# Four sets of chunk buffers, a bonus added by TensorE, staged rows of r, and one block a chunk in a recurrent-attention and two-layer kernel

## The chip, the core and the metric

The kernel runs on one core of a Trainium2 chip. The time is device microseconds of that core, and lower is better. A page and a trace of one profiled execution of the kernel before are at hand. The engines are called PE (TensorE), DVE (VectorE), ACT (ScalarE), POOL (GpSimd) and SP (SyncE, which here issues nearly all DMAs).

## The reference

Three stages in fp32: a linear recurrence over 768 tokens in 4 batches and 8 heads of 48, then two dense layers over the 3072 rows that it gives.

```python
B, H, S, D = 4, 8, 768, 48
for t in range(S):
    kt, vt, rt = k[:, :, t], v[:, :, t], r[:, :, t]
    cur = einsum('bhd,bhe->bhde', u[None] * kt, vt)          # the bonus of the token itself
    y[:, :, t] = einsum('bhd,bhde->bhe', rt, state + cur)
    state = w[None, :, :, None] * state + einsum('bhd,bhe->bhde', kt, vt)
x = y as rows (3072, 384)
x = ((x @ w1) * (x @ w2)) @ w3 @ w_mid                        # 384 -> 1024 -> 384
h = x @ w_in                                                  # 384 -> 1024
solu = h * softmax(h)
ln = (solu - mean) / sqrt(var + 1e-6) * g_ln
out = ln @ w_out                                              # 1024 -> 384
```

## The kernel before, in words

**Chunks.** The recurrence is cut into 24 chunks of 128 tokens; chunk n holds tokens of batch n % 4, and four chunks make a group c (0 to 5). For a chunk, r and k come transposed (`rT`, `kT`, loads "R" and "K", 48 x 512 each in two DMAs) and k and v by rows ("k" and "v"). `prep_R` and `prep_K` scale them by powers of w (`tab`). `a_chunk` (PE) multiplies them to a 128 x 128 matrix per head, and DVE copies the causal half of it into the tile `asb` under a mask ("ev", `copy_predicated`). On the diagonal of `asb` stands the bonus, one number per token and head. It is made in two ways: for chunks 0 to 8 (`n < NR`) DVE or POOL multiplies the transposed tiles (`prep_rk`), PE sums them with u (`bonus_mm`), and ACT copies the eight sums out; for later chunks POOL multiplies rows of r by u and k (`prep_ru`, `prep_ruk`), and DVE sums them (`bonus`). `diag` then writes the bonus into the diagonal of `asb`, on DVE or ACT. `y_chunk` (PE) multiplies `asb` by v and, from the second group on, adds r times the state; ACT and DVE split the result into a high and a low half ("yh", "yl") for exact products later. `st_chunk` (PE) and DVE advance the state.

**Dense layers.** Every fp32 product of the layers is three fp32r matmuls of high and low halves (`mm3`, L165 to L167). `s1_a` and `s1_b` give one 128-wide slice ft of the two products with w1 and w2 for the four chunks of a group (nine 512-column matmuls each), `s2` (nine again) multiplies their product by wc = w3 @ w_mid, which `w3_out` makes on the chip in eight parts "W". A second phase (from the first `ps_h` on) runs the second layer.

**Weights.** 24 units of weights are converted into halves on the chip. Each takes seven instructions on ACT, DVE and POOL (the functions from `cv_m` to `cv_h`, and `split`), of which DVE mostly has three (L429, L439, L448).

**Order.** Up to the end of the second group (`NG = 2`) a small planner, class `Plan`, orders all work: it holds a cost and a set of predecessors for each named step, starts the step that can start first, and breaks ties by the longest way to the end plus a bonus from the table `PRI`. Where PE would be idle before the first `s1_a`, it puts matmuls that compute nothing (`keep_warm`, L562). Each engine then works through its own list in order. After that, from c = 2 on, loops written by hand run `s1_a`, `s1_b`, `s1_gh`, `s1_gl`, `s2` for each ft, and `slot` puts the two halves of a chunk between them, in every ft one: an even slot has `bonus`, `diag`, `a_chunk`, an odd one `y_chunk` and `st_chunk`.

**Buffers.** There are two sets of `kT`, `rT` (`kTs`, `rTs`), so the loads of chunk n wait until chunk n - 2 has been used, two tiles `asb` up to chunk 8 and one after it, two staging buffers for weight units (`CB`), and a tile pair `wch`, `wcl` for wc that stands empty until the first part W.

Of the kernel before, what the change touches and what calls it, by code (L numbers as in the profile page):

```python
# [104 lines left out]
def tile_rwkv_bilinear_solu(  # L105
# [15 lines left out]
    g_ln: bass.AP,  # L121
    out: bass.AP,
# [22 lines left out]
    wch = const.tile([P, KF, DM], F32R, name="wch")  # L145
    wcl = const.tile([P, KF, DM], F32R, name="wcl")
# [47 lines left out]

    def flush():
        while later:
            later.pop(0)()


    def load_chunk(n, which="KRkrv"):  # L200
# [3 lines left out]
        for nm in which:  # L204
            if nm in T_d:
                src, tiles, dst = T_d[nm]
                t = dst[n] = tiles[n % len(tiles)]
                for o in range(2):
                    nc.sync.dma_start(t[o * DP:o * DP + D], src[b, c, o])
            else:  # L210
                if nm == "r" and not rows:
# [3 lines left out]
                    uall = u.rearrange("h d -> (h d)").partition_broadcast(P)  # L215
                    nc.sync.dma_start(rows["u"], uall.rearrange("p (h d) -> p h d", h=H))
# [14 lines left out]
    def prep_ru(n, e=nc.gpsimd):  # L231
        e.tensor_mul(rkv[n, "r"], rkv[n, "r"], rows["u"])
# [14 lines left out]
    def bonus_mm(n):  # L247
# [9 lines left out]
        later.append(evac)  # L257
# [5 lines left out]
    def asb_of(n):  # L263
        return asbs[n % 2 if n < N2 else 0]
# [47 lines left out]
    def y_chunk(n):  # L312
# [6 lines left out]
        for m, (hs, es) in enumerate(cuts):  # L319
            if c > 0:  # L320
                for j in range(HQ):
# [7 lines left out]
                    )  # L329
            if m < KM - 1:  # L330
                for j in range(HQ):
                    h = hs.start + j
                    nc.tensor.matmul(
                        ps[j * E0:(j + 1) * E0, m, :], lhsT=vt[:, h, es], rhs=asb_of(n)[:, h, :], start=c == 0, stop=True
                    )
            else:
                for o in range(2):
                    for j in range(NP):
# [3 lines left out]
                            start=c == 0 and o == 0, stop=o == 1,  # L342
# [4 lines left out]
    def st_chunk(n):  # L347
# [5 lines left out]
        ps = psa.tile([P, NP, D], F32, name="ps_s", tag="psa")  # L353
# [159 lines left out]
    def w3_out(ft):  # L513
# [3 lines left out]
        return split(ps, wch[:, ft, :], wcl[:, ft, :])  # L517
# [31 lines left out]
    for i, t in enumerate(kTs + rTs):  # L549
        (nc.vector if i % 2 else nc.gpsimd).memset(t, 0.0)  # L550
    nc.vector.memset(u2, 0.0)
    for o in range(2):
        nc.scalar.dma_start(
            u2[o * DP:o * DP + D, :, o], u.rearrange("(p o) d -> o d p", o=2)[o], allow_slow_non_contiguous=True
        )

    make_identity(nc, ident)
# [7 lines left out]
    nc.vector.memset(kpad[1], 0.0)  # L565
# [674 lines left out]
```

## Time and profile before

| | |
|---|---|
| median of 3 runs | 678.31 us (676.22 to 678.32) |
| the profiled execution | 679.14 us, of which the span from first to last instruction is 677.4 us |
| mean granted TensorE clock | 0.997 |
| PE busy | 665.0 us, 98% |
| DVE, ACT, POOL busy | 404.9, 299.3 and 252.0 us |

The profiled execution lies 0.83 us above the median. Busy PE counts the matmuls that compute nothing too, and a matmul's end is modelled, so 98% says where the limit is and not that PE does useful work all that time. An fp32 matmul of 128 columns shows as two records in the trace and as one row in the order of instructions.

### The profile page before, as it was taken

The numbers are of one execution on the slowest core, as the hardware profiler recorded it, in microseconds if no ns is written. First come the engines' busy times: TensorE is split into PE (matmuls) and PEld (weight loads), VectorE is DVE, ScalarE is ACT, GpSimd is POOL, SyncE is SP. The second block draws the span as 40 slices with busy tenths as digits, with TensorE's granted clock in tenths as the row PEclk, the third lists the DMA queues.
The fourth block names the chain that finished last, engine by engine and source line by source line (L and its number), as shares of the span: only waits on it lengthen the run. The fifth ranks groups of instructions, "written<-read, shape, count | busy, mean of one in ns | idle before, by whom it ended". The sixth has DMA issues, their size and how long they took to land.

```text
span 677.4 us, 12433 instructions
## 1 busy us (share of the span) xinstructions
PE 665.0 (98%) x4828; PEld 567.0 (84%) x4828; DVE 404.9 (60%) x730; ACT 299.3 (44%) x625; POOL 252.0 (37%) x253
## 2 busy tenths in 40 slices
PE   8999999999999999999999999999999999999996
PEld 8888778997777888888877887878999999999996
DVE  7798996666665433333344276537666666676653
ACT  3567965662322222322242366444544444444442
POOL 4576743331003455555584356332211222211210
PEclk9899999999999999999999999999999999999999
DMA  6567786453443122222121233000000000000001
GB/s 174 189 218 251 229 263 209 159 187 93 141 135 97 59 66 68 67 82 62 59 72 19 109 130 117 0 1 13 24 24 13 24 24 24 25 23 25 13 24 39
DMA packets 43379, 60.13 MB, mean 89 GB/s; under 512 B 6193, under 2 KB 31794, under 8 KB 43314
## 3 DMA queue, kind: packets, MB, share of 16 engines
q1 hardware_dynamic: 42898, 59.27, 27.8%
q8 instruction: 40, 0.66, 0.4%
q14 instruction: 25, 0.20, 0.1%
q10 hardware_dynamic: 416, 0.00, 0.0%
HBM read 50.34 MB, written 8.91 MB: 87 GB/s over the span
## 4 chain that ended last, share of the span: by engine, by line
PE 72%; DVE 8%; DMA 5%; POOL 5%; ACT 5%; issue 3%; SPq 0%; DVEq 0%; POOLq 0%; ACTq 0%
PE ps_h L165 5%; PE ps_h L167 5%; PE ps_h L166 5%; PE ps_o L167 5%; PE ps_o L166 5%; PE ps_o L165 5%; PE ps_x L165 4%; PE ps_bb L165 4%; PE ps_x L167 3%; PE ps_x L166 3%; PE ps_p L810 3%; PE ps_aa L165 3%; POOL cvm L433 3%; PE ps_bb L167 3%; PE ps_bb L166 3%
## 5 line engine op out<-in xcount | busy, mean ns | idle before, releaser
L647 POOL TENSOR_TENSOR gl<-g,gh 128x512 fp32r<-128x512 f32 x32 | 50.2, 1570 | 104.2 <-ACT gh L642 93.7
L433 POOL TENSOR_TENSOR cvm<-cvm,cvq 128x384 int32<-128x384 int32 (+1 forms) x54 | 64.3, 1197 | 58.8 <-ACT cvq L420 31.4
L788 POOL TENSOR_TENSOR rs<-vs,nhalf 128x1 f32<-128x1 f32 x24 | 13.0, 541 | 171.9 <-DVE vs L786 171.9
L165 PE MATMUL ps_o<-woh,pt 128*128 128x384 f32 x192 | 64.3, 335 | 0.0
L166 PE MATMUL ps_o<-wol,pt 128*128 128x384 f32 x192 | 64.3, 335 | 0.0
L167 PE MATMUL ps_o<-woh,pt 128*128 128x384 f32 x192 | 64.2, 334 | 0.0
L165 PE MATMUL ps_bb<-x,w2h 128*128 128x512 f32 x144 | 59.3, 412 | 0.0
L165 PE MATMUL ps_h<-wih,x2h 128*128 128x512 f32 x144 | 58.6, 407 | 0.7 <-ACT x2c L678 0.7
L769 ACT ACTIVATE e<-ps_h,nm 128x1024 f32<-128x1024 f32 x24 | 26.8, 1117 | 73.3 <-DVE nm L766 73.3
L165 PE MATMUL ps_aa<-x,w1h 128*128 128x512 f32 x144 | 58.1, 403 | 0.2
L636 DVE TENSOR_TENSOR g<-ps_bb,a 128x512 f32<-128x512 f32 x48 | 33.0, 687 | 40.7 <-PE ps_bb L167 40.7
L165 PE MATMUL ps_x<-gh,wch 128*128 128x512 f32 x144 | 57.0, 396 | 0.0
L167 PE MATMUL ps_x<-gh,wcl 128*128 128x512 f32 x144 | 56.3, 391 | 0.5 <-DVE wcl L448 0.5
L279 ACT COPY a<-ps_aa 128x512 f32<-128x512 f32 x44 | 25.6, 582 | 70.3 <-PE ps_aa L167 68.9
L167 PE MATMUL ps_h<-wih,x2l 128*128 128x512 f32 x144 | 56.6, 393 | 0.0
L167 PE MATMUL ps_bb<-x,w2l 128*128 128x512 f32 x144 | 56.4, 392 | 0.0
L167 PE MATMUL ps_aa<-x,w1l 128*128 128x512 f32 x144 | 56.3, 391 | 0.0
L166 PE MATMUL ps_bb<-x,w2h 128*128 128x512 f32 x144 | 56.3, 391 | 0.0
L166 PE MATMUL ps_aa<-x,w1h 128*128 128x512 f32 x144 | 56.2, 390 | 0.0
L166 PE MATMUL ps_h<-wil,x2h 128*128 128x512 f32 x144 | 56.2, 390 | 0.0
L166 PE MATMUL ps_x<-gl,wch 128*128 128x512 f32 x144 | 56.1, 390 | 0.0
L766 DVE TENSOR_REDUCE nm<-ps_h 128x1 f32<-128x1024 f32 x24 | 29.4, 1224 | 38.8 <-PE ps_h L167 38.8
(147 smaller groups left out, 1577.4 us busy)
## 6 DMA issues: line engine op xcount, KB each, us to landing
cvs<-in_w_T_dram SPq DMA_DIRECT2D x16, 512.0 KB, 4.1
cvs<-in_w_dram SPq DMA_DIRECT2D x16, 384.0 KB, 4.0
kT<-in_k_T_dram SPq DMA_DIRECT2D x48, 96.0 KB, 2.5
rT<-in_r_T_dram SPq DMA_DIRECT2D x48, 96.0 KB, 2.7
v_in<-in_v_dram SPq DMA_DIRECT2D x24, 192.0 KB, 3.0
k_in<-in_k_dram SPq DMA_DIRECT2D x24, 192.0 KB, 2.5
out_dram<-o SPq DMA_DIRECT2D x24, 192.0 KB, 1.8
gd<-g SPq DMA_DIRECT2D x16, 256.0 KB, 3.2
```

The source lines that it names most:

```text
L165: nc.tensor.matmul(dst, lhsT=ah, rhs=bh, start=start and i == 0, stop=False)
L166: nc.tensor.matmul(dst, lhsT=ah, rhs=bl, start=False, stop=False)
L167: nc.tensor.matmul(dst, lhsT=al, rhs=bh, start=False, stop=stop and i == last)
L279: (e.copy if e is nc.scalar else e.tensor_copy)(dst, src)
L433: nc.gpsimd.tensor_tensor(mi, mi, q, op=ALU.add)
L636: nc.vector.tensor_mul(gt[c, ft], pb, at[c, ft])
L647: e.tensor_sub(gl, g, f32(gh))
L766: nc.vector.tensor_reduce(out=nm, in_=ph, axis=AX.XY, op=ALU.max, negate=True)
L769: nc.scalar.activation(e, ph, AF.Exp, bias=nm, scale=1.0, accum_out=sm)
L788: nc.gpsimd.tensor_tensor(rs, vs, pq[0]["nhalf"], op=ALU.pow)
L810: nc.tensor.transpose(ps[:, j, :], pv[:, kf * P:(kf + 1) * P], ident)
```

## The change

Line numbers in the order of instructions are those of the respective file: L298 `a_chunk`, L251 `bonus_mm`, L356 `st_chunk`, L327, L333, L340 `y_chunk`, L562 `keep_warm`, L273 `diag`, L302 ev before are L361, L299, L425, L390, L401, L408, L635, L336, L365 after. L397 (identity times `vb`) and L308 (`vb`) are new. The tile named `early` is the area that holds all the early tiles.

1. **Four sets.** An area `early`, which later becomes wc (tag "wx"), holds two more sets of `kT`, `rT`, two more `asb`, and small tiles. Chunks below `NE = 8` rotate over four sets; the parts W may start only when chunks 0 to 7 and the bonus sums of chunks 5 to 8 are done (`free`).
2. **Bonus by TensorE.** For chunks 0 to 3 (`NV = 4`) there is no `diag`: DVE multiplies v by the eight sums from `bonus_mm` (two instructions, `evac_v`), and `y_chunk` adds the product with twelve matmuls against the identity.
3. **Rows of r for chunks 5 to 8.** `NR` goes from 9 to 5, so these four chunks take the way of the later ones, with r and u by rows in `early`.
4. **Staging and start.** Three staging buffers (`CB = 3`); w and u come as one small laid-out input `wu` in one DMA in place of four, the tiles are cleared by other engines in another order, `pw` moves into `early`, and `zero` is a tile of its own (before, it was an element of `rT1`, whose load so waited for ACT's clearing).
5. **One block a chunk** in the loops from c = 2 on: `block` does `y_chunk` and `st_chunk` of chunk n and `bonus`, `diag`, `a_chunk` of chunk n + 1 in one place, after `s1_gl` of every second ft (of every ft in c = 4); `st_chunk` takes the PSUM tile of `ps_aa`.
6. Other numbers in the planner's table, so another order up to the end of the second group.

```diff
-PRI = {'W.0': 20, **{f'yl{n}': 400 - 20 * n for n in range(4)}, **{f'st{n}': 310 for n in range(4)}}
+PRI = {
+    'W.0': 20, 'yl0': 503, 'yl1': 388, 'yl2': 393, 'yl3': 341, 'st0': 289, 'st1': 406, 'st2': 386, 'st3': 283, 'l_22': 37,
...
-CB = 2
+CB = 3
-NR = 9
-W0 = 19
+NR = 5
+NV = 4
+NT = 0
+NQ = 9
+NE = 8
+W0 = 15
+T0 = 8.1
...
+    early = const.tile([P, 2 * KF * DM], F32, name="early", tag="wx")
...
+    def open_wc():
+        if not wc:
+            t = const.tile([P, 2, KF, DM], F32R, name="wc", tag="wx")
+            wc["h"], wc["l"] = t[:, 0], t[:, 1]
...
+    for i in range(2):
+        kTs.append(early_tile(NP, P))
+        rTs.append(early_tile(NP, P))
...
+    def slot(n):
+        return n % 4 if n < NE else n % 2
...
-                t = dst[n] = tiles[n % len(tiles)]
+                t = dst[n] = tiles[slot(n)]
...
+        def evac_v():
+            vb = vbs[n % 2].rearrange("p h d -> p (h d)")
+            for es in (slice(0, E0), slice(E0, D)):
+                nc.vector.tensor_mul(
+                    vb[:, H * es.start:H * es.stop].rearrange("p (h d) -> p h d", h=H), rkv[n, "v"][:, :, es],
+                    ps.unsqueeze(2).to_broadcast([P, H, es.stop - es.start]),
+                )
...
-        later.append(evac)
+        later.append(evac_v if n < NV else evac)
...
+            elif n < NV:
+                vb = vbs[n % 2].rearrange("p h d -> p (h d)")
+                for j in range(HQ):
+                    lhsT = vb[:, (m * HQ + j) * E0:(m * HQ + j + 1) * E0]
+                    nc.tensor.matmul(ps[j * E0:(j + 1) * E0, m, :], lhsT=lhsT, rhs=ident, start=True, stop=False)
...
+    def block(n):
+
         flush()
...
+        more = n + 1 < NCH
+        if more:
+            bonus(n + 1)
+        y_chunk(n)
+        st_chunk(n, psf.tile([P, NP, D], F32, name="ps_s", tag="ps_aa"))
+        flush()
+        if more:
+            diag(n + 1)
+            a_chunk(n + 1)
+            prep_vrem(n + 1)
+            prep_state(n + 1)
+            flush()
+        load_chunk(n + 3, "Kkrv")
+        load_chunk(n + 2, "R")
+        prep(n + 2)
...
+    free = [f"{x}{n}" for n in range(NE) for x in "YS"] + [f"red{n}" for n in range(NR, NQ)]
...
-            f"W.{ft}", {"T": 4.25}, ready["m"] + ready["w"][2 * ft:2 * ft + 2] + [f"W.{ft - 1}"], wout,
+            f"W.{ft}", {"T": 4.25}, ready["m"] + ready["w"][2 * ft:2 * ft + 2] + [f"W.{ft - 1}"] + free, wout,
...
             s1_a(c, ft)
             flush()
-            mid()
+            if late:
+                cvstep()
             s1_b(c, ft)
             flush()
             s1_gh(c, ft)
             s1_gl(c, ft)
+            if cn < NCH and (ft % 2 == 0 or c == NC - 2):
+                block(cn)
+                cn += 1
```

The first place is PE's list just before the first matmul of the dense layers, `ps_aa`. Before, chunks 2 and 3 stand there with idle-time matmuls (`ps_warm`) between them:

```order
L562 MATMUL ps_warm<-ident 128x128 x12
...
L251 MATMUL ps_b<-u_79,rk 128x2 x4
L562 MATMUL ps_warm<-ident 128x128 x3
L333 MATMUL ps_y<-asb,v_in 32x128 x8
L340 MATMUL ps_y<-asb,vrem 32x128 x8
...
L562 MATMUL ps_warm<-ident 128x128 x7
L356 MATMUL ps_s<-v_in,kpad_84 64x48 x8
...
L356 MATMUL ps_s<-v_in,kpad_85 64x48 x8
L251 MATMUL ps_b<-u_79,rk 128x2 x4
L165 MATMUL ps_aa<-x,w1h 128x512
```

After the change the same stretch, from the bonus sums of chunk 3 to the first `ps_aa`, has the identity matmuls and no `ps_warm`:

```order
L299 MATMUL ps_b<-wv,rk 128x2 x4
L397 MATMUL ps_y<-ident,early 32x128 x4
L401 MATMUL ps_y<-early,v_in 32x128 x4
...
L408 MATMUL ps_y<-early,vrem 32x128 x8
L425 MATMUL ps_s<-v_in,kpad_84 64x48 x8
L425 MATMUL ps_s<-v_in,kpad_83 64x48 x8
...
L425 MATMUL ps_s<-v_in,kpad_84 64x48 x8
L191 MATMUL ps_aa<-x,w1h 128x512
```

Over the whole list up to the first `ps_aa` the rows of `ps_warm` go from 56 to 26 matmuls, and `y_chunk` of chunks 0 to 3 from 16 matmuls to 28. From there to the first `ps_h`, `ps_b` goes from 16 matmuls (four chunks) to none, and nothing else changes in number.

The second place is DVE's list at chunk 1, ahead of the first weight unit. Before, `diag` (L273) and a product for chunk 2 stand between two masked copies:

```order
L302 COPY_PREDICATED asb<-mask,ps_a_259 128x4x128
L273 COPY_PREDICATED asb<-ident,s 128x1024
L229 TENSOR_TENSOR kpad_84<-k_in,tabk 128x8x48
L243 TENSOR_TENSOR rk<-kT_82,rT_80 128x512
L448 TENSOR_TENSOR x<-ps_y,x 128x3x128
L302 COPY_PREDICATED asb<-mask,ps_a_325 128x4x128
```

After, `vb` (L308) stands in its place, and both products of chunk 2 with the table come early, on tiles of the third set:

```order
L365 COPY_PREDICATED asb<-mask,ps_a_253 128x4x128
L291 TENSOR_TENSOR rk<-early 128x512
L308 TENSOR_TENSOR early<-v_in,ps_b 128x256
L308 TENSOR_TENSOR early<-v_in,ps_b 128x128
L271 TENSOR_TENSOR early<-early,tab 128x512
L274 TENSOR_TENSOR early<-early,tab 128x512
L519 TENSOR_TENSOR x<-ps_y,x 128x3x128
L365 COPY_PREDICATED asb<-mask,ps_a_323 128x4x128
```

Up to the low half of chunk 3 (`yl3`), which the first `ps_aa` needs, DVE's list loses three rows of `diag`, one `rk` and one weight half (L448), and gains one product with the table and four pairs of L308. From there to the last weight half that the first part W needs it goes from 108 instructions to 122, among them four sums over rows of r; PE's list in the same stretch goes from 20 slices of the dense layer (`s1_a` or `s1_b`) to 23.

The third place is PE's list in the hand-written loop. Before, the two halves of a chunk stand apart, each between dense matmuls:

```order
L167 MATMUL ps_aa<-x,w1l 128x512
L327 MATMUL ps_y<-rT_80,spad 32x128 x4
...
L356 MATMUL ps_s<-v_in,kpad_84 64x48 x8
L165 MATMUL ps_bb<-x,w2h 128x512
...
L167 MATMUL ps_aa<-x,w1l 128x512
L298 MATMUL ps_a_3293<-rT_81,kT_83 128x128
...
L165 MATMUL ps_bb<-x,w2h 128x512
```

After, they are one run of fp32 matmuls between `ps_bb` and `ps_x`:

```order
L193 MATMUL ps_bb<-x,w2l 128x512
L390 MATMUL ps_y<-rT_79,spad 32x128 x4
...
L425 MATMUL ps_s<-v_in,kpad_83 64x48 x8
L361 MATMUL ps_a_3271<-rT_80,kT_82 128x128
...
L191 MATMUL ps_x_2722<-gh,wc 128x512
```

Between the first `ps_aa` and the first `ps_h` the runs of fp32 matmuls (chunk work) between fp32r ones go from 49 to 37: from the third group on from 23 to 12, ahead of it from 26 to 25. Everything from the first `ps_h` on stands in the same order as before.

## Rows read from the trace of the kernel before

**Rows 1.** Page: span, busy time, and PE in 40 equal slices.
```profile
span 677.4 us, 12433 instructions
PE 665.0 (98%) x4828; PEld 567.0 (84%) x4828; DVE 404.9 (60%) x730; ACT 299.3 (44%) x625; POOL 252.0 (37%) x253
...
PE   8999999999999999999999999999999999999996
```

**Rows 2.** Stretches: busy us of each engine (instructions), granted clock, DMA share, GB/s.
```profile
8.77:37.57 28.80, 27.38 (x382) 24.88 (x381) 23.45 (x42) 13.34 (x40) 15.27 (x13) 0.94 0.68 209
37.57:101.00 63.43, 62.99 (x618) 49.66 (x618) 59.29 (x111) 48.96 (x130) 41.18 (x39) 1.00 0.77 240
37.57:445.77 408.20, 406.19 (x3200) 331.36 (x3200) 232.60 (x378) 178.66 (x409) 190.90 (x157) 1.00 0.38 118
445.77:677.40 231.63, 225.06 (x1219) 204.39 (x1217) 143.42 (x289) 103.04 (x170) 41.38 (x71) 1.00 0.06 22
```

**Rows 3.** Timeline of PE to the first dense matmul: start, us, operation, [idle before].
```profile
2.36 7.19 PE L562 MATMUL ps_warm<-ident 128*128 128x128 f32 x38 [2.36 <-POOL ident masks.py:199]
...
20.14 1.02 PE L251 MATMUL ps_b<-u,rk 128*128 128x2 f32 x8 [1.42 <-DVE rk L243]
...
24.65 3.14 PE L562 MATMUL ps_warm<-ident 128*128 128x128 f32 x24
...
32.69 1.83 PE L562 MATMUL ps_warm<-ident 128*128 128x128 f32 x14
...
37.57 0.48 PE L165 MATMUL ps_aa<-x,w1h 128*128 128x512 f32 x1
```

**Rows 4.** Timeline of PE around one `a_chunk` and one `bonus_mm`.
```profile
43.37 0.39 PE L166 MATMUL ps_aa<-x,w1h 128*128 128x512 f32 x1
43.59 0.39 PE L167 MATMUL ps_aa<-x,w1l 128*128 128x512 f32 x1
43.91 1.16 PE L298 MATMUL ps_a<-rT,kT 64*128 64x128 f32 x16
45.00 0.50 PE L165 MATMUL ps_bb<-x,w2h 128*128 128x512 f32 x1
45.34 0.39 PE L166 MATMUL ps_bb<-x,w2h 128*128 128x512 f32 x1
...
47.18 0.95 PE L251 MATMUL ps_b<-u,rk 128*128 128x2 f32 x8
47.99 0.49 PE L165 MATMUL ps_aa<-x,w1h 128*128 128x512 f32 x1
```

**Rows 5.** Timeline of DVE to the first dense matmul.
```profile
8.77 0.69 DVE L243 TENSOR_TENSOR rk<-kT,rT 128x512 f32<-128x512 f32 x1
...
11.87 1.30 DVE L273 COPY_PREDICATED asb<-ident,s 128x1024 f32<-128x1024 int32 x1
13.07 1.75 DVE L223 TENSOR_TENSOR kT<-kT,tab 128x512 f32<-128x512 f32 x1
...
19.30 0.69 DVE L243 TENSOR_TENSOR rk<-kT,rT 128x512 f32<-128x512 f32 x1 [1.57 <-DMA rT<-in_r_T_dram]
19.91 0.55 DVE L448 TENSOR_TENSOR x<-ps_y,x 128x384 fp32r<-128x384 f32 x1
...
22.67 0.35 DVE L362 TENSOR_TENSOR st<-ps_s,w 128x192 f32<-128x192 f32 x1
...
28.92 1.34 DVE L302 COPY_PREDICATED asb<-mask,ps_a 128x512 f32<-128x512 int32 x2 [1.93 <-PE ps_a L298]
```

**Rows 6.** Waits of SP's DMA queue up to 40 us: total, times, longest.
```profile
SPq L209 <- PE ps_a L298: 6.8, 4, 3.3
...
SPq L209 <- ACT vrem L279: 2.1, 1, 2.1
```

**Rows 7.** Timeline of POOL up to 21 us.
```profile
12.09 2.17 POOL L226 TENSOR_TENSOR rT<-rT,tab 128x512 f32<-128x512 f32 x1 [6.67 <-DVE rk L243]
...
20.07 1.27 POOL L223 TENSOR_TENSOR kT<-kT,tab 128x512 f32<-128x512 f32 x1 [4.39 <-DVE rk L243]
```

**Rows 8.** Timeline of POOL in the loop, the first and last of one chunk's five products.
```profile
241.47 1.29 POOL L223 TENSOR_TENSOR kT<-kT,tab 128x512 f32<-128x512 f32 x1
...
246.01 1.06 POOL L235 TENSOR_TENSOR r_in<-r_in,k_in 128x384 f32<-128x384 f32 x1
```

**Rows 9.** Page, DMA issues: KB each, median us to landing.
```profile
rT<-in_r_T_dram SPq DMA_DIRECT2D x48, 96.0 KB, 2.7
```

More of the change, by code (lines that the diff above doesn't have):

```diff
@@ L121, in tile_rwkv_bilinear_solu @@
     g_ln: bass.AP,
+    wu: bass.AP,
     out: bass.AP,
@@ L193, in tile_rwkv_bilinear_solu, with same @@
     later, rows, rowx = [], {}, ExitStack()
+    def slot(n):
+        return n % 4 if n < NE else n % 2
+    def same(n):
+        return max([m for m in range(n) if slot(m) == slot(n)], default=-1)
     def flush():
@@ L231, in prep_ru @@
     def prep_ru(n, e=nc.gpsimd):
-        e.tensor_mul(rkv[n, "r"], rkv[n, "r"], rows["u"])
+        e.tensor_mul(rkv[n, "r"], rkv[n, "r"], rows_e[2] if n < NQ else rows["u"])
     def prep_ruk(n, e=nc.gpsimd):
@@ L255, in evac, with kpad_mm @@
             copy(e, bon[n], ps)
-        later.append(evac)
+        def evac_v():
[6 more added lines that the diff above has]
+        later.append(evac_v if n < NV else evac)
+    def kpad_mm(n):
+        ps = psf.tile([P, NP, P], F32, name="ps_k", tag="ps_bb")
+        for p in range(NP):
+            nc.tensor.transpose(ps[:, p, :], kT[n][:, p, :], ident)
+        later.append(lambda e: copy(e, kpad[n % 2].rearrange("t (p o) d -> t p (o d)", o=2), ps))
     def bonus(n):
@@ L352, in st_chunk @@
         kp, vt = kpad[n % 2], rkv[n, "v"]
-        ps = psa.tile([P, NP, D], F32, name="ps_s", tag="psa")
+        if ps is None:
+            ps = psa.tile([P, NP, D], F32, name="ps_s", tag="psa")
         for h in range(H):
@@ L548, in tile_rwkv_bilinear_solu, with clear @@
     nlim = NU
[L549 to L555, printed above, removed]
+    def clear(e, *tiles):
+        for t in tiles:
+            if e is nc.scalar:
+                nc.scalar.copy(t, zero.unsqueeze(2).to_broadcast(list(t.shape)))
+            else:
+                e.memset(t, 0.0)
+    clear(nc.vector, kTs[0], rTs[0])
+    clear(nc.gpsimd, kTs[1], rTs[1])
+    clear(nc.scalar, kTs[2], rTs[2], kTs[3], rTs[3])
     make_identity(nc, ident)
@@ L996, in tile_rwkv_bilinear_solu @@
             )
-    prio = dict(PRI, **{f"l_{i}": UB * (NU - i) for i in range(NU)})
+    prio = dict({f"l_{i}": UB * (NU - i) for i in range(NU)}, **PRI)
     todo = plan.order(3, prio, {f"A{n}": f"Y{n - 1}" for n in range(1, NA)})
-    clock, idle = 8.8, True
+    clock, idle = T0, True
     for t, name, e, end, fn in todo:
@@ L1210, in rows @@
         return _np.concatenate([x.reshape(-1, FF) for x in (a[0:4, 0:32], a[4:8, 0:32], a[:, 32:])])
+    wu = _np.zeros((2, 64, 3, H // 2), i["w"].dtype)
+    wu[:, :, 0] = 1
+    wu[:, :D, 0] = i["w"].reshape(H // 2, 2, D).transpose(1, 2, 0)
+    wu = wu.reshape(2, 64, 3 * (H // 2))
+    for o in range(2):
+        wu[o, :D, H // 2 + o::2] = i["u"].reshape(H // 2, 2, D)[:, o].T
     laid = {
```

151 lines of the change are left out of this document (74 added, 77 removed), and 3 rows, old and new, of the table PRI.

## The prediction

> **What bounds the kernel now.** I read the page first: PE is busy 98% of the span, in nearly every slice [rows 1], so nothing that DVE, ACT or POOL does later than the start can matter unless it makes PE wait. The stretches say where PE is the limit. From the first dense matmul at 37.57 us to the second phase at 445.77 PE is busy 406.19 of 408.20 us; the second phase takes the remaining 231.63 us and is not touched [rows 2]. Only the 37.57 us before the first `ps_aa` are not PE's: there much of its busy time is `ps_warm`, which computes nothing, 38 records at the start, 24 at 24.65, 14 at 32.69 [rows 3]. The end is thus the sum of two things: when the first `ps_aa` starts, and how much PE has to do from there to the end.
>
> What holds the first `ps_aa` back is the chain of chunks 0 to 3, mostly on DVE: in the 28.80 us from its first product at 8.77 to the first dense matmul DVE is busy 23.45 [rows 2]. Two of its waits carry most of the other 5.35 us: 1.57 for the load of `rT` of chunk 2, and 1.93 for the `a_chunk` that follows from it [rows 5]. The load itself was late because SP held it behind `a_chunk` of an earlier chunk, which was reading the same buffer: 6.8 us in four waits, and 2.1 us more behind ACT's clearing [rows 6].
>
> **The start.** The sum goes against the profiled execution (679.14 us, 0.83 over the median); the result is taken off the median.
>
> The single load of w and u: two SP issues become one of 12 columns, and the clearing is spread. I take 0.4 us (one SP issue of two), between 0 and 0.8. DVE's first product then starts at 8.4.
>
> DVE's work from there to `yl3`: three `diag` of 1.30, one `rk` of 0.69 and one weight half of 0.55 leave, one product of 0.68 comes [rows 5], which is 4.5 less. The four pairs that make `vb` are not in the trace. They read PSUM, 256 and 128 columns; the nearest rows that do so have 384 columns (0.55) and 192 (0.35) [rows 5]. On the line through these two, 256 columns take 0.42 and 128 take 0.28, so a pair takes 0.70, between 0.55 (if broadcasting costs nothing and the small one less than the line) and 0.90; four are 2.8. DVE so does 23.45 - 4.5 + 2.8 = 21.75 us. `diag` is replaced on PE by twelve matmuls in each of four `y_chunk`, in all 96 records of some 0.06 us by the 128-column `a_chunk` (16 in 1.09 us, [rows 4]): 6.5 us of PE time, but in place of `ps_warm`, which had at least 24 and 14 records in 3.14 and 1.83 us there [rows 3]. They cost nothing as long as DVE is later than PE; without that cover they would cost the 6.5 us.
>
> Waits: with four sets the loads of chunks 2 and 3 wait for no matmul, so the 1.57 goes, and with it most of the 1.93 and of the waits for sums that follow. I keep 0.8 of the 5.35 for the latency from PE to DVE. The first `ps_aa` then comes at 8.4 + 21.75 + 0.8 = 31.0 in place of 37.57: **6.6 us earlier**. Ends: all of the waiting stays (35.5, 2.1 earlier), or none and no POOL collision either (29.1, 8.5 earlier).
>
> **PE's work after the start.** Four `bonus_mm`, for chunks 5 to 8, leave: from 47.18 to the next matmul at 47.99 one takes 0.81 [rows 4], four take **3.2 us**. What takes their place (rows of r times u and k, and a sum) goes to POOL and DVE; POOL is busy 41.18 of 63.43 us there and the DMA queues have a share of 0.77 [rows 2], so five more loads of 192 KB lie beside other work.
>
> Switching between fp32r and fp32 matmuls costs PE time. Within a slice a matmul starts 0.22 to 0.23 after the last. The last one before `a_chunk` holds PE for 0.32 (43.59 to 43.91), and the first one after it for 0.34 (45.00 to 45.34) [rows 4]: 0.2 us for each run of chunk work between dense matmuls. There are 12 fewer such runs, 11 of them in the loop, where the two halves of a chunk become one: **2.4 us**. Nothing is added on PE. The cover for the other edits of the loop is PE's own queue: `st_chunk` now takes the tile of `ps_aa`, which the next `s1_a` writes, but nine `s2` matmuls stand between, and the sum that empties the tile takes 0.35 on DVE [rows 5].
>
> **What is given back.** Up to 101 us, shortly before the first part W, DVE was already busy 59.29 of 63.43 us [rows 2]; its list there grows from 108 instructions to 122, at the same mean to 67.0 us. PE has three slices more (27 matmuls of 0.23) and four `bonus_mm` and two switches less: 63.4 + 6.2 - 3.6 = 66.0. So both are full, DVE by 1.0 us more than PE, and any wait of DVE can become a wait of PE. The bounds: nothing (if DVE's new instructions are shorter than its mean), or the 1.0 and all of the 4.1 us that DVE idled in that stretch, 5.1. I take **1.5 us**, nearer to nothing, since the parts W only move behind slices that PE has ready. That W must wait for the last reader of `early` is hidden by the same slices.
>
> Sum: 6.6 + 3.2 + 2.4 - 1.5 = 10.7 us. 679.14 - 10.7 = 668.4, and against the median of 678.31: **667.5 us**.
>
> **Rivals.**
>
> *DVE and POOL block each other.* POOL's product at 12.09 took 2.17 us where a like one takes 1.27 [rows 7], and DVE's product beside it took 1.75 against 0.69 [rows 5]: 1.06 us of DVE lost in one meeting. In the new order POOL has `rk` and products for chunks 1 to 3 while DVE has six products that read two SBUF tiles. By the Trainium skill (SBUF — State Buffer, section "SBUF: two separate sides") DVE and GpSimd take a shared pair of ports as an exclusive lock, against each other when DVE reads two SBUF inputs and GpSimd reads SBUF too; the pair of rows above agrees with it. That speaks against a plan that moves work to POOL. Three meetings more cost 3.2 us of the start, and in the full stretch behind it the 5.1 us would go whole: 6.6 - 3.2 + 5.6 - 5.1 = 3.9 us, **674.4 us**. Against it: only one of DVE's products met POOL in this way before.
>
> *The start is bound by something else.* If `a_chunk`, the weight units or the loads keep DVE waiting as long as before, the first `ps_aa` comes at 35.5: 2.1 + 5.6 - 1.5 = 6.2 us, **672.1 us**. A PE that idles before the first `ps_aa` belongs here: after the pause of 1.42 us at 20.14 [rows 3] the granted clock of the whole stretch was 0.94 [rows 2], and such a fall costs more if it falls on dense matmuls.
>
> *All pauses go.* If the start reaches its lower end, nothing is given back and the 2.0 us in which PE is idle up to 445.77 [rows 2] vanish: 8.5 + 5.6 + 2.0 = 16.1 us, **662.2 us**.
>
> *The block makes PE wait (slower).* In `block` the sum over r of chunk n + 1 stands on DVE ahead of the low half of `y` and of the sum that empties the `ps_aa` tile, and it waits for POOL's last product of that chunk. Those five products take 5.6 us (241.47 to 247.07, [rows 8]) and follow a load of `rT` that lands in 2.7 us [rows 9] and is issued at the end of the block before; the last is so ready some 7.5 us after it. In c = 2 and 3 the next block is two ft away (over 12 us), so there is slack; in c = 4 it is one ft away (27 matmuls of 0.23, 6.2 us), so DVE waits 1.3 us, while PE needs the tile only after the block and `s2`, over 5 us later. From 11 us of waiting on, 1 us in each of 11 blocks, the gain is gone; at 1.5 us in each the time would be 667.5 + 16.5 = **684 us**.
>
> **How the numbers follow.** The forecast's own range is 663.5 to 671, chance 0.57. DVE against POOL 0.17, the start bound elsewhere 0.10, all pauses gone 0.09, slower 0.04, 0.03 is left for a time near no change. The range of 8 in 10 goes from 661 to 674. About 0.3% (2 us) is what a measurement here can tell from no change: faster by more 0.92, within it 0.04, slower 0.04.
>
> **What would show it.** The first `ps_aa` at 30 to 32 us; DVE busy some 22 us from its first `rk` to there with under 2 us of waits, none for a load of `rT`; no `diag` on DVE before it; pairs of L308 at 0.7 us. From the first `ps_aa` to the first `ps_h` about 404 us in place of 408.2, and from there to the end 231.6 as before. It would be wrong if PE shows pauses between 31 and 100 us that end with DVE, or in the loop before `ps_aa` behind `ps_s`, or if the first `ps_aa` comes after 34 us.

## The result and the profile after

The kernel after takes 668.72 us (median of 4 runs, 667.36 to 670.17), the kernel before on the same chip 677.26 (675.64 to 678.32): ratio 0.9864, 95% interval 0.9834 to 0.9893. The profiled execution took 670.03 us. One execution among those below, 679.35 us of h0, lies over 1.5% above the fastest of its kernel and is left out of h0's ratio.

The page of the kernel after (span, busy time) stands against [rows 1]:

```profile
span 668.2 us, 12402 instructions
PE 653.4 (98%) x4832; PEld 558.6 (84%) x4832; DVE 410.2 (61%) x727; ACT 299.1 (45%) x616; POOL 267.4 (40%) x274
```

PE is still the limit. It is busy 11.6 us less, but `ps_warm` is part of that; from the first `ps_aa` to the first `ps_h` it is busy 400.87 us in place of 406.20. The stretches of the kernel after, in the columns of [rows 2], cut at DVE's first product (10.01), the first `ps_aa` (32.58), the first part W (`ps_wc`, 98.94) and the first `ps_h` (436.39):

```profile
10.01:32.58 22.57, 21.55 (x418) 19.67 (x418) 21.28 (x45) 9.83 (x27) 15.47 (x13) 1.00 0.76 230
32.58:98.94 66.36, 64.19 (x617) 49.95 (x614) 60.33 (x114) 53.47 (x139) 54.83 (x52) 0.97 0.87 269
98.94:436.39 337.45, 336.68 (x2554) 278.83 (x2553) 177.79 (x260) 126.89 (x272) 149.38 (x125) 1.00 0.29 93
436.39:668.20 231.81, 225.06 (x1219) 204.39 (x1217) 143.40 (x289) 103.03 (x170) 41.41 (x71) 1.00 0.06 21
```

The same cuts in the kernel before, whose first W starts at 102.09:

```profile
37.57:102.09 64.52, 64.08 (x622) 50.54 (x622) 60.34 (x113) 49.00 (x131) 41.18 (x39) 1.00 0.77 242
102.09:445.77 343.68, 342.12 (x2579) 280.82 (x2578) 172.26 (x266) 129.66 (x279) 149.72 (x118) 1.00 0.30 95
```

The 9.2 us of the two spans are therefore 4.99 from an earlier first `ps_aa`, 1.84 lost up to W, 6.23 won from W to `ps_h`, and 0.18 lost behind it. The gain is about as large as forecast, but the start gave less than forecast, and the stretch up to W is longer, although PE has less work there by the count below. These two places are read more closely.

**The start.** DVE's timeline of the kernel after, to be read against [rows 5]:

```profile
5.75 1.86 DVE L661 COPY tab<-early 128x4 f32<-128x4 f32 x1
7.64 2.38 DVE L664 TENSOR_TENSOR tab<-tab,early 128x8 f32<-128x8 f32 x7
9.94 0.16 DVE L667 COPY w<-early 128x4 f32<-128x4 f32 x1
10.01 0.68 DVE L291 TENSOR_TENSOR rk<-kT,rT 128x512 f32<-128x512 f32 x1
...
12.01 0.62 DVE L308 TENSOR_TENSOR early<-v_in,ps_b 128x256 f32<-128x256 f32 x2
13.39 0.69 DVE L271 TENSOR_TENSOR kT<-kT,tab 128x512 f32<-128x512 f32 x1 [0.77 <-POOL rk L291]
...
15.23 1.49 DVE L291 TENSOR_TENSOR rk<-early 128x512 f32<-128x512 f32 x1
...
17.18 0.97 DVE L271 TENSOR_TENSOR early<-early,tab 128x512 f32<-128x512 f32 x1
```

And POOL's beside it:

```profile
5.75 1.84 POOL L625 MEMSET early<- 128x1024 f32 x2
...
15.18 2.42 POOL L277 TENSOR_TENSOR kpad<-k_in,tabk 128x384 f32<-128x384 f32 x2
```

A copy of 4 columns (L661) takes 1.86 us, one of the same shape at 9.94 takes 0.16. It starts with POOL's clearing of two tiles and ends with it. DVE's first product so comes at 10.01 and not at 8.4 as forecast, nor at 8.77 as before. From there the chain goes as forecast: no `diag`, no wait for a load, 22.57 us to the first `ps_aa`, of which DVE is busy 21.28 and waits 1.29. The products at 15.23 and 17.18 are slowed beside POOL's at 15.18 (1.49 and 0.97 us where 0.68 is usual).

**Up to W.** PE's timeline around the only long pause:

```profile
43.87 0.40 PE L193 MATMUL ps_bb<-x,w2l 128*128 128x512 f32 x1
46.43 1.25 PE L361 MATMUL ps_a<-rT,kT 64*128 64x128 f32 x16 [2.17 <-POOL cvm L504]
47.61 0.50 PE L191 MATMUL ps_aa<-x,w1h 128*128 128x512 f32 x1
...
48.64 0.63 PE L191 MATMUL ps_aa<-x,w1h 128*128 128x512 f32 x1
49.07 0.63 PE L192 MATMUL ps_aa<-x,w1h 128*128 128x512 f32 x1
```

POOL's and DVE's timelines just ahead of it, in one fence each, and the load of the rows of k from the view of DMA issues of 34 to 46 us (KB, us to landing):

```profile
42.46 1.02 POOL L283 TENSOR_TENSOR early<-early,k_in 128x384 f32<-128x384 f32 x1 [1.46 <-DMA kT<-in_k_T_dram]
```

```profile
43.51 0.55 DVE L324 TENSOR_REDUCE s<-early 128x8 f32<-128x384 f32 x1 [0.98 <-POOL early L283]
...
44.91 1.31 DVE L271 TENSOR_TENSOR kT<-kT,tab 128x512 f32<-128x512 f32 x1
```

```profile
k_in<-in_k_dram SPq DMA_DIRECT2D x1, 192.0 KB, 6.5
```

The matmuls are those of `a_chunk` of chunk 5. The row names POOL's `cvm`; the operand that came just ahead of them is `kT`, which DVE finished at 46.22. DVE was late because the sum over the staged rows of r of chunk 5 (L324) stood ahead of it and waited for POOL's product with k (L283), and POOL waited for a load. The row names a load of `kT`, but the operand of L283 that comes from a load is the rows of k: that load was issued at 35.80 and took 6.5 us, so it landed at 42.3, just before L283 started. DVE's product for `kT` then took 1.31 us beside POOL's `cvm` where 0.69 is usual. Behind the pause PE's matmuls start 0.43 us apart in place of 0.23. The clock of these microseconds:

```profile
48.00:49.00 1.00, 1.00 (x4) 0.81 (x3) 1.00 (x3) 0.80 (x3) 1.00 (x3) 0.58 0.96 334
...
50.00:51.00 1.00, 1.00 (x4) 0.59 (x2) 0.53 (x2) 0.00 (x0) 1.00 (x2) 0.50 0.90 253
```

The granted clock was at its lower level of 1.2 GHz. The nine matmuls took 3.7 us (47.61 to 51.33) in place of 2.1. So in this execution the one pause cost 2.17 and about 1.6 us.

### The profile page after: what moved, and what is told of

It is laid out like the page before. It is cut to its first block, busy times and chain, and to the rows that moved or that the text cites. A ratio compares the mean times of both kernels' runs of the same rounds, so it can differ in the third digit from the quotient of the medians.

```text
span 668.2 us, 12402 instructions
## 1 busy us (share of the span) xinstructions
PE 653.4 (98%) x4832; PEld 558.6 (84%) x4832; DVE 410.2 (61%) x727; ACT 299.1 (45%) x616; POOL 267.4 (40%) x274
## 3 DMA queue, kind: packets, MB, share of 16 engines
HBM read 51.33 MB, written 8.91 MB: 90 GB/s over the span
## 4 chain that ended last, share of the span: by engine, by line
PE 79%; DVE 5%; DMA 5%; POOL 4%; ACT 4%; issue 2%; SPq 0%; DVEq 0%; POOLq 0%; ACTq 0%
PE ps_h L191 5%; PE ps_h L193 5%; PE ps_h L192 5%; PE ps_o L192 5%; PE ps_o L193 5%; PE ps_o L191 5%; PE ps_x L191 4%; PE ps_x L193 4%; PE ps_x L192 4%; PE ps_aa L191 4%; PE ps_aa L193 4%; PE ps_aa L192 4%; PE ps_bb L191 4%; PE ps_bb L192 3%; PE ps_bb L193 3%; PE ps_p L879 3%
## 5 line engine op out<-in xcount | busy, mean ns | idle before, releaser
L504 POOL TENSOR_TENSOR cvm<-cvm,cvq 128x384 int32<-128x384 int32 (+1 forms) x54 | 67.4, 1255 | 39.1 <-DVE cvm L500 28.4
L716 POOL TENSOR_TENSOR gl<-g,gh 128x512 fp32r<-128x512 f32 x32 | 41.2, 1288 | 63.0 <-ACT gh L711 63.0
L191 PE MATMUL ps_x<-gh,wc 128*128 128x512 f32 x144 | 58.2, 404 | 0.0
L191 PE MATMUL ps_bb<-x,w2h 128*128 128x512 f32 x144 | 57.2, 398 | 0.0
L193 PE MATMUL ps_x<-gh,wc 128*128 128x512 f32 x144 | 56.3, 391 | 0.0
L192 PE MATMUL ps_x<-gl,wc 128*128 128x512 f32 x144 | 56.1, 390 | 0.0
L192 PE MATMUL ps_bb<-x,w2h 128*128 128x512 f32 x144 | 56.1, 390 | 0.0
```

Of the source, the lines that this page charges most:

```text
L191: nc.tensor.matmul(dst, lhsT=ah, rhs=bh, start=start and i == 0, stop=False)
L192: nc.tensor.matmul(dst, lhsT=ah, rhs=bl, start=False, stop=False)
L193: nc.tensor.matmul(dst, lhsT=al, rhs=bh, start=False, stop=stop and i == last)
L504: nc.gpsimd.tensor_tensor(mi, mi, q, op=ALU.add)
L716: e.tensor_sub(gl, g, f32(gh))
```

## Experiments

Twelve measurements, in three batches; every ratio is to the kernel before in the same batch.

**The start: the block on DVE, and the clock.** The kernel after again, as the control of the first batch:

> The changed kernel itself, as the measure for the other three runs of this call. Theory: the first dense matmul at 32.6 us, PE waits some 2.2 us ahead of the matmul of chunk 5 (a_chunk) near 44 us, and in some executions the granted clock falls after that wait, which splits the times in two groups some 2.6 us apart (667.4 and 670.1 in its four runs). Rival: the two groups have nothing to do with this wait.

Measured: 670.66 us (668.10 to 677.03, 10 runs), ratio 0.9899 (0.9863 to 0.9935); first `ps_aa` at 33.07 in its profile. Its PE waits 2.19 us ahead of chunk 5, and the clock behind that stays at 1.00. Five of the ten took 668.1 to 669.6 at a mean clock of 0.997 to 1.0, the others 671.8 to 677.0 at 0.984 to 0.993. That spread had not been in the first four runs, and its cause was open.

Now the two tiles are cleared by ACT:

```diff
-    clear(nc.scalar, asbs[1], vrem, spad, kpad[1])
+    clear(nc.scalar, asbs[1], vrem, spad, kpad[1], asbs[2], asbs[3])
...
-    clear(nc.gpsimd, asbs[2], asbs[3])
```

> Two of the early tiles asb are cleared by ACT at the end of its clearing and no longer by POOL. Theory (POOL's clearing held DVE's copy into tab for 1.86 us where it takes 0.17, so the whole start came 1.7 us late): the copy takes 0.2, DVE's first product starts at 8.3 in place of 10.0, the first dense matmul at 30.9 in place of 32.6, the time falls by 1.7 us against the changed kernel. Rival (the start is bound by the loads or by the weight units that the first dense matmul needs): the copy is short but the first dense matmul stays within 0.5 us of 32.6.

Measured: 668.37 us (667.30 to 668.99, 4 runs), ratio 0.9862 (0.9835 to 0.9890). DVE's timeline:

```profile
5.75 0.16 DVE L660 COPY tab<-early 128x4 f32<-128x4 f32 x1
...
8.32 0.69 DVE L291 TENSOR_TENSOR rk<-kT,rT 128x512 f32<-128x512 f32 x1
```

The copy takes 0.16, and the first product stands at 8.32, 1.69 us earlier: the long copy was the meeting with POOL. The first `ps_aa` comes at 31.62, so 0.96 of the 1.69 arrive there; the rest goes into a wait of 1.54 us at 28.37 ahead of chunk 3's `y_chunk`, for ACT's and DVE's halves of x. In time the two intervals overlap, so the gain of some 1 us is shown by the traces and not by the medians. All four runs had a clock of 0.997 or more. This kernel is called e1 below and is what the edits of the later batches stand against; it was itself measured in the first batch only.

Is the wait ahead of chunk 5 what spreads the clock? 18 matmuls that compute nothing were put ahead of that `a_chunk`:

```diff
+        if n == 5:
+            for i in range(18):
+                nc.tensor.matmul(pso[0][:, i % NP, :], lhsT=ident, rhs=ident, start=True, stop=True)
```

> 18 matmuls of the identity, which compute nothing that is kept, stand ahead of a_chunk of chunk 5, where PE waited 2.17 us for the scaled kT. They need neither rT nor kT. Theory (the wait let the granted clock fall for 3.3 us behind it): the clock stays at its upper level from 48 to 52 us, nine matmuls of the slice behind take 2.1 us in place of 3.7, and no execution is in the upper group: some 1.6 us less than the upper group (670 to 668.4), or 667.4 if the wait itself shrinks too. Rival (the fall has another cause, or comes wherever it wants): the clock falls all the same, the time stays.

Measured: 671.17 us (670.67 to 673.94, 4 runs), ratio 0.9901 (0.9876 to 0.9926). No gain. Its profiled execution was the one of 673.94 us, and there the clock fell in another place, at the start. Two stretches, two rows of PE and one of DVE:

```profile
8.00:10.00 2.00, 0.00 (x0) 0.00 (x0) 1.83 (x7) 0.00 (x0) 0.00 (x0) 0.98 0.86 264
10.00:18.00 8.00, 7.91 (x48) 7.46 (x49) 4.65 (x11) 0.48 (x1) 4.27 (x4) 0.58 0.67 200
```

```profile
10.09 1.12 PE L675 MATMUL ps_t<-ident,tab 128*128 128x128 f32 x4 [2.15 <-DVE tab L667]
...
36.39 0.50 PE L191 MATMUL ps_aa<-x,w1h 128*128 128x512 f32 x1
```

```profile
13.60 0.62 DVE L308 TENSOR_TENSOR early<-v_in,ps_b 128x256 f32<-128x256 f32 x2 [1.56 <-PE ps_b L299]
```

PE idles 2.15 us until DVE's late table is there, then its clock is 0.58 from 10 to 18 us. DVE waits 1.56 us for PE's sums, and the first `ps_aa` comes at 36.39, 3.8 us later than in the kernel after. The kernel after has the same idle stretch (from 8.3 to 10.08 us, 1.81 us), as has e0 (2.54 us to 10.09), and in their profiles the clock behind it stays at 1.00: the same start falls in one execution and not in another. The next kernel bridges that stretch with matmuls that compute nothing:

```diff
-W0 = 15
+W0 = 27
```

> The kernel after (cleared tiles still on POOL) with 27 calls in place of 15 for the first ps_warm, which bridge the stretch from 8.3 to 10.1 us in which PE idles there; nothing else differs. Theory (the runs of the kernel after at 672 to 677 us, with a mean granted clock of 0.982 to 0.993, are those in which the granted clock fell behind that idle stretch): DVE's first product stays at about 10.0 us and the first ps_aa at 32.6 to 33.1, but no run has a mean clock under 0.995 and none takes over 671.5 us; median 668.5 to 669.5, ratio 0.987. Rival (the clock varies for another reason, such as the wait ahead of a_chunk of chunk 5): some of the runs still show 0.982 to 0.993 and 672 to 677 us.

> The kernel after, unchanged, as the partner of h1. Theory (in some executions the granted clock falls behind the stretch from 8.3 to 10.1 us in which PE idles): among its runs some with a mean clock of 0.982 to 0.993 and 672 to 677 us, as in e0 (5 of 10 there), the others at 667 to 670.5. Rival (that spread belonged to one batch only): all runs at 667 to 671 us.

> The kernel after with 27 calls in place of 15 for the first ps_warm, again, in more runs. Theory (the filled stretch keeps the clock): no run with a mean clock under 0.995, none over 671.5 us, while h0 has such runs. Rival: as many slow ones as h0.

Measured: g1 668.99 us (668.76 to 670.85, 4 runs), ratio 0.9878 (0.9846 to 0.9909); h1 668.46 (666.50 to 669.84, 6 runs), 0.9854 (0.9829 to 0.9879); no clock under 0.996 in the ten. Beside h1, on the same chip, the unchanged kernel h0 took 667.38, 668.20 and 668.62 at clocks of 0.996 to 0.999, and 674.62, 677.04 and 679.35 at 0.990, 0.985 and 0.981 (median 671.62; ratio 0.9897, 0.9850 to 0.9945). Filling the idle stretch kept the clock in all ten runs, though DVE's first product was still late (first `ps_aa` at 32.84 and 33.60). The expectation of a control that spreads and a filled kernel that doesn't was met; the numbers of runs are small.

**The staged rows of r.** With `NR = 6` chunk 5 takes its bonus from TensorE again:

```diff
-NR = 5
+NR = 6
```

> Chunk 5 makes its bonus by PE again (NR = 6), so only chunks 6 to 8 take rows of r. The planner orders anew, with one bonus_mm (0.8 us) and one run of chunk work (0.2 us) more on PE after the start. Theory (PE waited at chunk 5 because DVE's product for kT stood behind the sum over rows of r, and that behind POOL's product and a late load of k): the wait of 2.2 us and the fall of the clock behind it go, 3.8 us, against 1.0 us of work: the stretch from the first dense matmul to the first part W, 66.4 us now, takes 2.8 us less per slice count, and the time is 1 to 3 us below that of the changed kernel. Rival (DVE as a whole is behind, whichever way the bonus comes): a wait of 2 us or more stands elsewhere before 60 us, and the time is equal or 1 us longer.

Measured: 672.69 us (667.97 to 676.86, 10 runs), ratio 0.9929 (0.9899 to 0.9958). In the profile, a run of 667.97, no pause stands ahead of chunk 5 and the first `ps_aa` to the first `ps_h` takes 401.1 us (after: 403.81). But the tiles are cleared by POOL here, and six of the ten runs had a clock of 0.982 to 0.992, so the median can't show the effect. The same edit on e1, where the start is clean:

> e1 (668.37 us, ratio 0.9862, 402.93 us from the first ps_aa to the first ps_h, of which 2.1 are the wait ahead of a_chunk of chunk 5) with the bonus of chunk 5 alone by TensorE again, so that the first staged rows of r are those of chunk 6. Theory (that wait comes from the rows of chunk 5, which land late): it is gone, and 402.9 - 2.1 + 0.81 + 0.2 = 401.8 us from the first ps_aa to the first ps_h, 667.3 us, ratio 0.985. Rival (PE then waits for another late engine in the same stretch, as it did with all four bonus_mm back): 403.5 us or more, 669 us or more.

Measured: 666.60 us (664.60 to 667.22, 6 runs), ratio 0.9824 (0.9801 to 0.9848), all at 0.998 or 0.999. Its stretches, cut as above:

```profile
30.98:98.08 67.10, 66.31 (x635) 51.58 (x632) 61.56 (x116) 51.83 (x134) 53.38 (x47) 1.00 0.81 255
98.08:433.28 335.20, 334.33 (x2545) 276.84 (x2544) 175.09 (x261) 126.70 (x274) 147.86 (x122) 1.00 0.30 95
```

PE's idle time up to W falls from 2.10 us in e1 (64.88 less 62.78, below) to 0.79, with one slice and one `bonus_mm` more in the stretch, and the first `ps_aa` to `ps_h` takes 402.30 us (expected 401.8, e1 402.93). This is the lowest median of all. Its interval lies wholly under 1 and just under that of h0 on the same chip (0.9850 to 0.9945); it overlaps those of h1, of e1 and of the first measurement of after, so that it is faster than these is not shown by the times.

All four `bonus_mm` back, on e1 (`NR = 9`):

> e1 (668.37 us, ratio 0.9862, 402.93 us from the first ps_aa to the first ps_h) with the bonus of chunks 5 to 8 by TensorE again (four bonus_mm of 0.81 us, no rows of r staged early). Theory (the four bonus_mm are worth 3.2 us and 0.2 for one more run of chunk work, and the wait of 2.1 us ahead of a_chunk of chunk 5 comes from the staged rows of r): no such wait, and 402.9 + 3.4 - 2.1 = 404.2 us from the first ps_aa to the first ps_h, 669.7 us, ratio 0.988. Rival A (the wait ahead of a_chunk of chunk 5 has another cause and stays): 406.3 us, 671.8 us. Rival B (work on POOL and DVE costs PE as much as the bonus_mm saved): 403 us or less, 668.4 us or less.

Measured: 672.50 us (672.09 to 672.88, 4 runs), ratio 0.9920 (0.9891 to 0.9949); 406.63 us from the first `ps_aa` to `ps_h`. The two stretches of e1, then the first of f2, two of the waits of f2's PE up to 120 us (in all, times, longest), and one of its `bonus_mm`:

```profile
31.62:96.50 64.88, 62.78 (x617) 48.91 (x614) 60.15 (x114) 53.85 (x140) 54.82 (x52) 1.00 0.88 276
96.50:434.55 338.05, 336.63 (x2554) 278.81 (x2553) 178.39 (x260) 126.46 (x270) 150.74 (x125) 1.00 0.29 92
```

```profile
32.19:97.49 65.30, 62.47 (x568) 50.07 (x565) 62.43 (x115) 46.40 (x115) 46.15 (x40) 0.97 0.77 239
```

```profile
PE ps_s L425 <- DVE x L519: 1.4, 1, 1.4
...
PE ps_s L425 <- POOL kpad L277: 1.0, 1, 1.0
```

```profile
58.89 0.95 PE L299 MATMUL ps_b<-wv,rk 128*128 128x2 f32 x8
59.70 0.48 PE L191 MATMUL ps_aa<-x,w1h 128*128 128x512 f32 x1
```

That is 3.7 us more than e1, where rival A had 3.4. The pause of chunk 5 is gone, as the theory had it, but others came in the same stretch, and the clock there is 0.97. So the total alone doesn't price the four `bonus_mm`: of the 3.7 us about 1.7 are the lower clock from 72 to 76 us (0.57 there). What prices them is the row: 0.81 us from 58.89 to the next matmul, as in [rows 4], so 3.2 for four. Set against e1 without idle time (3.52 us there, 3.05 here) and without that fall, f2's PE has about 2.5 us more to do, not 3.4; what makes the difference is open. With the four back PE still waits in that stretch: of my theory the first half holds by the rows, and the second did not hold. The pause goes without another in its place in f7 and in the profile of `NR = 6` before it (0.64 us of idle time up to W).

**One block a chunk.** The two half slots of the kernel before, in the loop of e1:

```diff
-            if cn < NCH and (ft % 2 == 0 or c == NC - 2):
-                block(cn)
-                cn += 1
+            step()
```

(`step` issues `a_chunk` of a chunk, or its `y_chunk` and `st_chunk`; 48 runs of chunk work between dense matmuls in place of 37.)

> The kernel after with the cleared tiles on ACT (as in e1, which is what this run stands against: 668.37 us, ratio to before 0.9862, first ps_aa to first ps_h 402.93 us) and with the loop's two half slots a chunk of the kernel before put back: 48 runs of chunk work between dense matmuls in place of 37, all other work the same. Theory (each run costs PE 0.2 us for switching between fp32r and fp32 matmuls): 402.93 + 11 x 0.2 = 405.1 us from the first ps_aa to the first ps_h, about 670.6 us, ratio 0.9895. Rival A (the switch is hidden, what one block saves is nothing): 402 to 403.5 us, 668.4 us. Rival B (the half slots also make PE wait, so the block saved more than the switches): over 406.5 us, 672 us or more.

Measured: 670.73 us (667.89 to 673.38, 4 runs), ratio 0.9881 (0.9844 to 0.9917). The stretches:

```profile
34.42:98.42 64.00, 64.00 (x615) 50.09 (x614) 59.01 (x112) 52.58 (x135) 53.12 (x51) 0.97 0.85 267
98.42:439.71 341.29, 339.62 (x2555) 278.00 (x2553) 171.09 (x260) 126.02 (x273) 157.25 (x125) 1.00 0.30 92
```

Together 405.29 us, 2.36 more than e1 (expected 405.1). That the total comes so close is partly luck: up to W, where both lists have the same runs, this profile lacks e1's idle time of 2.10 us and has a lower clock (0.59 from 34.42 to 38.42, about 1.6 us) that e1 has not. The price is read from W to `ps_h`, where all 11 runs more lie and the clock is 1.00 in both: PE is busy 339.62 us in place of 336.63, 2.99 more or 0.27 for each run, and idle 0.25 us more. So the theory held, with a price of 0.27 rather than 0.20. This profile's start lost 2.8 us on its own (a wait of 2.7 us for x, and a clock of 0.93 over 8 to 34.42 us), so the time spreads widely; the trace tells the theory from its rivals, the medians alone do not.

**Bonus by TensorE for chunks 0 to 3, and the four sets.** First `NV = 0` on e1, which brings `diag` back:

```diff
-NV = 4
+NV = 0
```

> e1 (first ps_aa at 31.62 us) with the bonus of chunks 0 to 3 by diag on DVE and ACT again; the four sets of buffers and the single load of w and u stay. Of the four diag two stand on DVE ahead of the first ps_aa (1.30 us each), and the four pairs on PSUM (0.61 each) are gone, with one product (0.69) and one product of kpad (0.54) added: 2.6 + 1.2 - 2.4 = 1.4 us more on DVE. Theory (DVE's work sets the start): first ps_aa 1 to 2 us later, 32.6 to 33.6 us, and 669.4 to 670.4 us. Rival A (most of the start's gain came with the diag, since chunks then wait for one another again): 34.5 us or later, 671.5 us or more. Rival B (the 96 small matmuls of the new bonus cost PE what DVE saves): 31.7 us or earlier, no change in the time.

Measured: 671.22 us (670.67 to 671.61, 4 runs), ratio 0.9902 (0.9873 to 0.9930); first `ps_aa` at 34.48, 2.86 us later than e1, at the edge of rival A, with 403.0 us behind it as in e1. The 1.4 us of work that I had counted leave something out; two rows of DVE show part of it:

```profile
20.98 1.68 DVE L336 COPY_PREDICATED early<-ident,s 128x1024 f32<-128x1024 int32 x1
22.55 1.75 DVE L271 TENSOR_TENSOR early<-early,tab 128x512 f32<-128x512 f32 x1
```

Two products of `kT` take 1.75 here (this one and one at 12.11) beside POOL, where 0.69 is usual: 2.1 us more, against 1.3 for the two products slowed in e1. The planner's order moves with the steps, so not all of the 2.86 is the price of `diag`.

Then two sets of `kT` and `rT` for all chunks:

```diff
     def slot(n):
-        return n % 4 if n < NE else n % 2
+        return n % 2
```

> e1 (first ps_aa at 31.62 us, 668.37 us, ratio 0.9862) with two sets of kT and rT for the first chunks too, as in the kernel before; bonus by TensorE, rows of r, one block a chunk stay. Theory (the loads of rT and kT then wait again for the matmuls of the chunk two before, as the waits of 1.57 and 1.93 us before did): first ps_aa 2 to 4 us later, 33.6 to 35.6 us, and 670.4 to 672.4 us. Rival (with the diag gone and another order the loads come in time anyway, and the four sets are worth nothing): first ps_aa before 32.6 us, 668 to 669.4 us.

Measured: 672.66 us (672.18 to 673.70, 4 runs), ratio 0.9921 (0.9892 to 0.9951). First `ps_aa` at 33.83, 2.2 later than e1, and 405.45 us from there to `ps_h`, 2.5 more. SP's timeline of this kernel, and of e1, shows when the load of `kT` of chunk 2 goes out:

```profile
11.94 0.80 SPq L252 DMA_DIRECT2D kT<-in_k_T_dram  x2
```

```profile
5.71 0.83 SPq L252 DMA_DIRECT2D early<-in_k_T_dram  x2
```

And the stretch up to W, with its longest wait:

```profile
33.83:101.51 67.68, 63.75 (x562) 49.00 (x558) 61.19 (x113) 46.93 (x116) 48.63 (x48) 0.97 0.76 244
```

```profile
84.52 0.41 PE L401 MATMUL ps_y<-early,v_in 128*32 128x128 f32 x2 [2.24 <-DVE early L365]
```

The load is 6.2 us later. DVE does not wait for it as before: the planner puts conversion of weights in between, and DVE's longest wait there is 0.86. PE idles 3.9 us up to W, 2.24 of them ahead of one `y_chunk`, and has a clock of 0.97 there where e1 has 1.00. The theory's range for the first `ps_aa` held, and the time lies just over its range; that the sets are worth as much again behind it, I had not expected. Whether the later loads are what PE waits for there was not taken apart.

## Why the prediction was right, and where it was not

**The start**: forecast 6.6 us earlier, measured 4.99. The terms of the sum:

- DVE's first product at 8.4: 8.32 with the clearing on ACT (e1), 10.01 as the change is written. This is the step that failed. The text put no cost on "the clearing is spread", and it cost 1.7 us: two clearings on POOL held up one copy of 4 columns at the head of DVE's chain. It is the rival *DVE and POOL block each other*, at a place that I did not look at, since I weighed it for products only. The Trainium skill (SBUF — State Buffer, section "SBUF: two separate sides") says that the shared ports are held for the whole of a GpSimd instruction against a DVE operation in a two-port mode too, and counts fp32 copies between SBUF tiles among these; the 1.86 us beside POOL's clearing, and 0.16 without it, agree.
- DVE's work of 21.75 and waits of 0.8, together 22.55: measured 21.28 and 1.29, together 22.57. Inside it the pairs of `vb` take 0.60 to 0.62 (forecast 0.70), and the meeting with POOL at 15.2 adds 1.1 us in return. Loads no longer made DVE wait, as forecast. In f4 and f5, without the sets or without the new bonus, the first `ps_aa` comes 2.2 and 2.9 us later than in e1; the planner's order changes with each, so these are not the prices of the two alone.
- The wait of 1.93 us in the kernel before, which the text lets follow from the late load of chunk 2, was read too simply. A stretch of that trace with its clock, three rows of PE, and DVE's product for `rT` of chunk 2:

```profile
20.00:26.00 6.00, 5.86 (x82) 5.35 (x83) 5.18 (x12) 4.61 (x15) 4.96 (x5) 0.72 0.49 151
```

```profile
16.12 0.65 PE L333 MATMUL ps_y<-asb,v_in 128*32 128x128 f32 x16
...
21.70 1.15 PE L333 MATMUL ps_y<-asb,v_in 128*32 128x128 f32 x16
...
27.73 1.16 PE L298 MATMUL ps_a<-rT,kT 64*128 64x128 f32 x16
```

```profile
22.07 0.68 DVE L226 TENSOR_TENSOR rT<-rT,tab 128x512 f32<-128x512 f32 x1
```

Both operands of that `a_chunk` were ready by 22.75 us (`kT`, from POOL, by 21.34 [rows 7]), but PE came to it at 27.73, behind `y_chunk` and `st_chunk` of chunk 1 and the 24 records of `ps_warm` at 24.65 [rows 3]. Behind its pause of 1.42 us at 20.14, for which the load was the cause, PE had a clock of 0.72 from 20 to 26 us: `y_chunk` and `st_chunk` took 2.95 us there (21.70 to 24.65), where like ones take 1.02 and 0.60 us at full clock. By an estimate from these rows some 1.3 of the 1.93 us are thus the lower clock of this one execution, which the profile of the kernel after doesn't have at its start. How much of the 4.99 us is owed to that and not to the change is open, since only one execution of the kernel before was profiled.

**PE's work after the start**: forecast 3.2 for four `bonus_mm` and 2.4 for 12 fewer switches. The rows of f2 bear out 0.81 us for one of the first, but the sum of its PE's work only about 2.5 in all; f3 gives 2.99 of PE's busy time for 11 of the second, so that term was a little too small. In kind both held.

**What is given back**: forecast 1.5 us up to W, with a count that was wrong. The text has PE's list there grow by three slices; in the order of instructions it grows by one, from 20 slices to 21. One `st_chunk` (0.6 us to the next matmul in e1's timeline of PE) comes in too. By that count the stretch should have gone from 64.52 to 64.52 + 2.05 (nine matmuls of 0.23) + 0.6 - 3.2 - 0.4 = 63.6 us. It took 66.36, so 2.8 were given back: the 2.17 of the pause and about 1.6 of the lower clock behind it, less the 0.44 that PE idled there before, make 3.3, 0.5 more than that. In e1, whose clock stays at 1.00, PE is busy 62.78 there, within 1 us of the corrected count, and idle 2.10. This is the second step that failed: that DVE and PE are both full was not the mechanism. DVE's busy time in the stretch, forecast to grow to 67.0 us, stayed as it was (60.34 before, 60.33 after). It was one chain of a load, POOL, DVE and PE, and with chunk 5's rows gone (f7) the pause was gone. The rows of r were costed at nothing as lying beside other work, and chunk 5's did not lie beside it.

**The sum** came out close because errors of opposite sign met: 1.6 less at the start and 1.3 more given back, against more than forecast from W to `ps_h`. Of the 6.23 us won there one slice (2.05), one `st_chunk` (0.6) and 10 switches at the 0.27 of f3 make 5.35, and 0.8 of PE's idle time went (1.56 before, 0.77 after), which I had not counted; that leaves 0.1.

**The rivals.** The block between DVE and POOL was real, in part. A PE that idles ahead of the first `ps_aa` and loses its clock, named under *the start is bound by something else*, goes with the executions of 671.8 us and more: 8 of 20 of the kernel after, none of 10 with that idle time filled. *All pauses go* did not happen: a new one came. *The block makes PE wait* did not happen: PE is idle 0.77 us in 337.45 from W on. From `ps_h` to the end nothing changed (231.63, 231.81).

**The signs.** DVE's work and waits, the missing `diag`, the pairs of L308 and the time from `ps_aa` to `ps_h` (403.81, forecast about 404) came as the text said they would. The first `ps_aa` at 32.58 lies outside its 30 to 32, and one of its signs of being wrong was there: the pause at 46.43 ends with DVE's `kT`.

## What to carry to other kernels

A clearing that is moved to POOL is not free if DVE's short copies run beside it: look at what stands at the head of the chain in those microseconds, not at the engine's load. A pause of PE costs its length and, in some executions, a stretch at the lower clock behind it. Matmuls that compute nothing removed the second cost at the start (g1, h1); the same ahead of chunk 5 gained nothing (e6), and there it helped to take one task off the chain (f7). When work is moved from a full engine to freer ones, leave out the first chunk if its data lands late: `NR = 6` in place of 5, with the clearing on ACT, gave 666.60 us. Before a total is taken as the price of an edit, see whether both profiles have the same pauses and the same clock.

## What was not expected of the hardware

One start has two courses. PE idles until 10.08 or 10.09 us, for 1.81 us in the kernel after, for 2.54 us in e0 and for 2.15 us in e6. Behind that the granted clock was 1.00 in the first two, the longer idle time among them, and 0.58 from 10 to 18 us in the third. The difference was 3.8 us at the first `ps_aa`, against 4.99 that the change gave there.

A copy of 4 columns waited through two POOL clearings in a row, 1.86 us: it did not get in between them.
